# Moving work between the stages of an attention, experts and dense kernel: second routing, first dense tile, early flag, new step order

## The chip, the cores and the metric

The kernel runs on one core of one Trainium2 chip. The metric is the device time of one execution in microseconds (us), the median of several runs. A profile, taken by the hardware profiler in one execution, shows every instruction of five engines: TensorE (PE; its weight loads are PEld), VectorE (DVE), ScalarE (ACT), GpSimd (POOL) and SyncE (SP, which issues most DMAs).

## The reference

Three parts follow each other; 3072 tokens (4 batches of 768) have 384 channels (8 heads of 48).

```
for t in range(S):                       # 1. attention: a complex decaying state per batch and head
    new_re = ar * S_re - ai * S_im       # ar, ai: a_re, a_im scaled to a magnitude of at most 0.999
    new_im = ar * S_im + ai * S_re
    S_re, S_im = new_re + outer(k[t], v[t]), new_im
    y[t] = q[t] @ S_re
logits = x @ w_gate + modality_bias[modality_id]      # 2. experts, one of 8 for each token
e_idx  = argmax(logits); gate_w = softmax(logits)[e_idx]
out[e_idx == e] = gate_w * (relu(x @ w1[e]) @ w2[e])  # 384 -> 1024 -> 384
h = ((x @ w1) * (x @ w2)) @ w3                        # 3. dense, 384 -> 1024 -> 1024
result = h @ w_out                                    # 1024 -> 384
```

The gate and bias weights of part 2 and all four weights of part 3 arrive as 64-bit floats.

## The kernel before

**Stage A, attention.** The sequence is cut into 24 chunks of 128 tokens (4 batches of 6). The decay's magnitudes and angles are prepared for groups of one or two chunks (`f_mag`, L180, and `f_ang`, L240): logarithm, exponential, arctangent and sine on ScalarE, and sums along the sequence as scans on VectorE (L214 for `ar`, L256 for `ai`), with a few products on GpSimd (L218, L261). A chunk itself is a list of 16 named steps, `STEPS`, written by hand: its scores (`sc0`, `sc1`), outputs (`y0`, `y1`) and the writing of its predecessor's rows (`out`, `lg`); for the next chunk the transposes of K and Q in two halves (`kt0`, `kt1`, `qt0`, `qt1`, all in `t_tr`, L320 to L331) and the state (`st1`, `st2`); for the chunk after that the products of q and k with the magnitudes (`mq`, `mk`) and with cosine and sine (`tc`, `ts`, in `t_rot`, L309, which reads the transposes `c` and `s` of L299). The program calls these steps in the list's order; a scheduler may move instructions on PE, DVE and SP within limits. Behind every step a queue of operations with due times is served: the next group's magnitudes and angles, loads, and the **routing** of the first half of the tokens.

**Routing** (`route`, L916) is a generator of 18 pieces. From the logits of 12 chunks it finds each token's expert (L932 to L940), counts tokens with two matmuls (`ct`, `rk`, L945, L946), works out where every token goes (L952 to L990), builds one-hot matrices (`ohB` L994, `ohBx` L997 on ScalarE and L998 on GpSimd, `ohA` L1004) and turns them into lists of row numbers with 12 matmuls (`perm`, L1008). The routing of half 0 is queued in chunk 12 from `R_A` to `R_B`, its names begin with `r0`. That of half 1 (`r1`) runs after the last chunk, in one go:

```
for _ in groups[1][0]:
    pass
g.g2 = g.cp.tile([P, NTILE], F32, name="g2")
setA()
gates(tc, g, g.pa, "", g.g2)
nc.vector.tensor_tensor(g.g2, g.g2, g.g2, ALU.mult)
```

`setA` loads ScalarE's table for exponentials, `gates` (L1017) computes `ex` and the gate factor `g`.

**Stage B, experts.** Each half has two items of 800 rows, each item two subs of 400 rows: 8 subs, the first four for half 0. A sub gathers its rows (`xg`, GpSimd's DMA), transposes them (`xt`, L444), splits them into a high part on ScalarE (`xh`, L445) and a low part on VectorE (`xl`, L446), and then has 8 steps `f`: `h(f)` is 9 matmuls (three terms for each of three slices, L456) with a relu and a split (`hh` L460, `hl` L461), `z(f-2)` 9 more (L474). `zev` takes the sums out, `otr` transposes them (`zo`, L488), copies them (`zr`, L490) and scatters them to a buffer in memory (`zs`, L491, GpSimd's DMA). The next item's weights are split into `wh` and `wl` (L513, L514). Beside that a list `work` of 42 items is popped by progress: 28 of `w34_work` (24 units converted from 64-bit floats, and w3 @ w_out as `w34p`), and 12 units that convert m1 and m2 (`conv_m`, L1206); the conversion is a chain of VectorE instructions (L805 to L818). A step counts as done 48 times (6 steps in each of 8 subs), and the pace is `total * done / (todo * 0.93)` with `todo` 48.

**Stage C, dense** (`c_stage`, L704). Six tiles of 512 tokens: `load` brings four blocks `cz` back from memory, `tr` transposes them (`czt`, L729; `czh` L730, `czl` L731), `ab(f)` computes both products (`ca`, `cb`, L743; `cat` L747, `cab` L749), `o` multiplies with the combined weight (`co`, L764), `ev` scales with the gate and stores.

**End** (`general`, L1327). Two conditions under which the fast path doesn't hold are put into one flag: `okp` (a matmul, a sum over all of `chk`), `fl`, `fi` (L1343), a load of the flag into a register on every engine (L1344), and a branch (L1345).

PSUM has 8 banks of 128 x 2 KB; in stages B and C four of them are the group `ps`, which `xt`, `h`, `zo`, `czt`, `ca` and `cb` share.

Of the kernel before, what the change touches and what calls it, by code (L numbers as in the profile page):

```python
# [55 lines left out]
R_A = 1.2  # L56
# [5 lines left out]
STEPS = ["sc0", "kt0", "mq", "out", "qt0", "sc1", "st1", "mk", "y0", "kt1", "lg", "tc", "y1", "ts", "st2", "qt1"]  # L62
# [519 lines left out]
def attention(tc, g):  # L582
    nc = tc.nc
    g.pa = g.left.enter_context(tc.tile_pool(name="pa", bufs=1, reuse_waits="tile"))
    g.bact = g.right.enter_context(tc.tile_pool(name="bact", bufs=1, side="right", reuse_waits="tile"))
# [66 lines left out]
    start, rest = b_stage(tc, g, groups, work)  # L652
# [51 lines left out]
def c_stage(tc, g):  # L704
    nc = tc.nc
    V, A, TE = nc.vector, nc.scalar, nc.tensor
    ps, pc = g.Cs, g.Cact
# [4 lines left out]
    def load(s):  # L712
        for t in range(CT // P):
            n = s * (CT // P) + t
            b = n // (GB * NCH)
            x = ps.tile([P, DM], F32, tag="zr", bufs=4, name=f"cz{n}")
            d = nc.sync.dma_start(out=x, in_=g.zsv[NRC * b][n * P:(n + 1) * P, :])
            for r in range(1, NRC):
                for q in g.scat[b][r]:
                    tc.add_manual_dep(d.ins, q.name, mybir.DependencyInfo(mybir.DependencyClass.Sync, mybir.DependencyReason.DATA), reason="rows scattered")  # L720
            zt[s, t] = x

    def tr(s):
        hi = ps.tile([P, NTH, CT], R, tag="zh", bufs=2, name=f"czh{s}")
        lo = ps.tile([P, NTH, CT], R, tag="zl", bufs=2, name=f"czl{s}")
# [8 lines left out]
    def ab(s, f):  # L734
# [45 lines left out]
    for s in range(ns):  # L780
        for f in range(1, NF):
            ab(s, f)
            o(s, f - 1)
            if f == 4 and s + 1 < ns:
                tr(s + 1)
                if s + 2 < ns:
                    load(s + 2)
        if s + 1 < ns:
            ab(s + 1, 0)
        o(s, NF - 1)  # L790
        ev(s)
# [124 lines left out]
def route(tc, g, pool, b0, b1, fx, cap, rows, nit, kc, nk_, idx, eid, nt, lidx=None):  # L916
# [81 lines left out]
    nc.gpsimd.tensor_tensor(Bx[:, :, 1, :], Bc, cst[:, C_TB + b0 * NCH:C_TB + b1 * NCH].unsqueeze(2).to_broadcast(shB), ALU.mult)  # L998
# [327 lines left out]
def general(tc, g):  # L1326
# [17 lines left out]
    anyf = nc.values_load(fi[0:1, 2:3], min_val=0, max_val=1)  # L1344
    with tc.If(anyf > 0):  # L1345
# [43 lines left out]
def build(ctx, tc, g):  # L1389
# [7 lines left out]
    with tc.tile_pool(name="Cw", bufs=1, reuse_waits="tile") as Cw:  # L1397
# [20 lines left out]
        g.right.close()  # L1418
        with tc.tile_pool(name="Cs", bufs=1, reuse_waits="tile") as Cs, tc.tile_pool(name="Cact", bufs=1, side="right", reuse_waits="tile") as Cact:
            g.Cs, g.Cact = Cs, Cact  # L1420
            c_stage(tc, g)
# [47 lines left out]
```

## Time and profile before

| | us |
|---|---|
| median of 3 runs | 936.71 (935.76 to 937.67) |
| the profiled execution | 936.86 |
| its span, first to last instruction | 935.0 |
| start-up, before the first chunk | about 0 to 37 |
| stage A with its 24 chunks | about 37 to 333.4 |
| between A and B | 333.4 to 343.8 |
| stage B | 343.8 to 609.3 |
| between B and C | 609.3 to 616.3 |
| stage C | 616.3 to 924.8 |
| end | 924.8 to 935.0 |

The bounds of the stages are those of PE's work: the last `lq` of a chunk, the first `h`, the last `z`, the first `ca`, the last `co`. A view of stretches gives for each the busy time of every engine and the TensorE clock that was granted, 1.00 being 2.4 GHz and 0.50 the lower level, 1.2 GHz. A time in brackets behind an instruction is how long its engine stood idle before it, and what ended that.

### The profile page before, as it was taken

To read this page: it belongs to the slowest core of one execution; us is meant where nothing else is said; L and a number is where in the kernel's file an instruction comes from. 1 tells how busy PE (TensorE), PEld (TensorE's weight loads), DVE (VectorE), ACT (ScalarE), POOL (GpSimd) and SP (SyncE) were. 2 spreads that over 40 slices of the span, in tenths; PEclk is the share of its full clock that TensorE was granted. 3 is DMA by queue.
4 is the path that set the end of the run, shared out by engine and by line. 5 is a ranking of instruction groups with operands and counts; after the bars stand their busy time and mean duration, and the time that the engine had idled before them with its cause. 6 is when DMAs were issued, how large, how long until landed. Compare 5 with 4: busy or idle time off the path is not lost.

```text
span 935.0 us, 14100 instructions
## 1 busy us (share of the span) xinstructions
PE 836.4 (89%) x5469; PEld 760.5 (81%) x5469; DVE 540.6 (58%) x953; ACT 420.6 (45%) x722; POOL 165.7 (18%) x136
## 2 busy tenths in 40 slices
PE   0559889887988969999999999989999999999995
PEld 0548778766777859899999999978888888888884
DVE  2658987889887669877782898223232232222222
ACT  4758888887786423432442443122222122222211
POOL 2213233233234221233231211110000000000000
PEclk9969999988889979999999999999999999999998
DMA  6513443434343334563451354111000010100001
GB/s 159 137 30 105 126 111 100 111 98 140 107 125 95 99 120 144 176 194 117 138 162 33 119 161 120 34 58 34 34 6 28 35 34 35 34 34 1 34 0 39
DMA packets 77951, 81.02 MB, mean 87 GB/s; under 512 B 25704, under 2 KB 70232, under 8 KB 77876
## 3 DMA queue, kind: packets, MB, share of 16 engines
q1 hardware_dynamic: 72324, 70.13, 25.7%
q0 software_dynamic: 5120, 9.70, 3.7%
q8 instruction: 45, 0.74, 0.3%
q14 instruction: 30, 0.25, 0.1%
q10 hardware_dynamic: 432, 0.20, 0.1%
HBM read 65.75 MB, written 14.44 MB: 86 GB/s over the span
## 4 chain that ended last, share of the span: by engine, by line
PE 60%; issue 13%; DVE 10%; POOL 5%; ACT 5%; DMA 2%; POOLq 0%; DVEq 0%; ACTq 0%; SPq 0%
PE ca L743 11%; PE co L764 11%; PE cb L743 11%; PE h L456 6%; PE z L474 6%; PE w34p L868 4%; DVE ar L214 2%; PE sc L364 2%; DVE ai L256 2%; POOL xg L434 1%; POOL zs L491 1%; PE tpk L326 1%; PE sp L340 1%; PE yT L381 1%; POOL ai L261 1%
## 5 line engine op out<-in xcount | busy, mean ns | idle before, releaser
L749 DVE TENSOR_TENSOR cab<-cb,cat 128x512 f32<-128x512 f32 x48 | 33.2, 692 | 182.1 <-PE cb L743 182.1
L747 ACT ACTIVATE cat<-ca 128x512 f32<-128x512 f32 x48 | 28.7, 598 | 123.0 <-PE ca L743 123.0
L752 ACT ACTIVATE cabh<-cab 128x512 fp32r<-128x512 f32 x48 | 30.3, 631 | 94.5 <-DVE cab L749 94.5
L456 PE MATMUL h<-xh,wh 128*128 128x400 f32 x192 | 68.5, 357 | 1.4 <-DVE xl L446 1.2
L456 PE MATMUL h<-xh,wl 128*128 128x400 f32 x192 | 66.8, 348 | 0.0
L456 PE MATMUL h<-xl,wh 128*128 128x400 f32 x192 | 66.8, 348 | 0.0
L474 PE MATMUL z<-hh,wh 128*128 128x400 f32 x192 | 66.8, 348 | 0.0
L474 PE MATMUL z<-hh,wl 128*128 128x400 f32 x192 | 66.5, 346 | 0.0
L474 PE MATMUL z<-hl,wh 128*128 128x400 f32 x192 | 66.1, 344 | 0.0
L460 ACT ACTIVATE hh<-h 128x400 fp32r<-128x400 f32 x64 | 32.2, 503 | 74.4 <-PE h L456 73.2
L764 PE MATMUL co<-w34h,cabl 128*128 128x384 f32 x192 | 65.1, 339 | 0.0
L764 PE MATMUL co<-w34h,cabh 128*128 128x384 f32 x192 | 65.0, 339 | 0.0
L764 PE MATMUL co<-w34l,cabh 128*128 128x384 f32 x192 | 65.0, 339 | 0.0
L491 POOL DMA_INDIRECT zs<-zr,idx x32 | 35.1, 1098 | 161.9 <-ACT zr L490 102.6
L364 PE MATMUL sc<-tq,tk 96*128 96x128 f32 x384 | 58.5, 302 | 0.2 <-ACT tq L331 0.2
L743 PE MATMUL ca<-czh,m1h 128*128 128x512 f32 x144 | 57.3, 398 | 0.4 <-ACT czh L730 0.4
L743 PE MATMUL ca<-czl,m1h 128*128 128x512 f32 x144 | 57.4, 399 | 0.0
L743 PE MATMUL ca<-czh,m1l 128*128 128x512 f32 x144 | 57.3, 398 | 0.0
L743 PE MATMUL cb<-czl,m2h 128*128 128x512 f32 x144 | 56.4, 392 | 0.0
L743 PE MATMUL cb<-czh,m2h 128*128 128x512 f32 x144 | 56.0, 389 | 0.0
L743 PE MATMUL cb<-czh,m2l 128*128 128x512 f32 x144 | 56.0, 389 | 0.0
L364 PEld LDWEIGHTS sc<-tq,tk 96*128 96x128 f32 x384 | 54.1, 218 | 0.9 <-ACT tq L331 0.8
(247 smaller groups left out, 2157.8 us busy)
## 6 DMA issues: line engine op xcount, KB each, us to landing
ws<-in_w SPq DMA_DIRECT2D x32, 384.0 KB, 4.6
w<-in_m3t SPq DMA_DIRECT2D x16, 512.0 KB, 4.1
v<-in_v SPq DMA_DIRECT2D x24, 256.0 KB, 3.1
m<-in_m SPq DMA_DIRECT2D x12, 512.0 KB, 4.1
q<-in_q SPq DMA_DIRECT2D x24, 192.0 KB, 2.6
k<-in_k SPq DMA_DIRECT2D x24, 192.0 KB, 2.6
xb<-xr SPq DMA_DIRECT2D x24, 192.0 KB, 2.2
cz<-zs SPq DMA_DIRECT2D x24, 192.0 KB, 3.5
```

The source lines that it names most:

```text
L214: V.tensor_tensor_scan(t["ar"], g.rst[:, :NTH * GROUPS[n][2] * P], t["s2"], 0.0, ALU.mult, ALU.add)
L364: nc.tensor.matmul(sc[:, j * P:(j + 1) * P], kt[:, j * P:(j + 1) * P], qt[:, j * P:(j + 1) * P], start=True, stop=True)
L456: TE.matmul(p[:, :SUB], lt[:, sl], rt[:, i, :], start=(n == 0), stop=(n == 3 * NTH - 1))
L460: A.activation(hh, p[:, :SUB], AF.Relu)
L474: TE.matmul(acc[j][:, :SUB], lt[:, sl], rt, start=(f == 0 and k == 0), stop=(f == NF - 1 and k == 2))
L491: d = G.indirect_dma_start(out=g.zsv[r_ * NRC + r], out_offset=bass.IndirectOffsetOnAxis(ap=idx[:, c0 + r:c0 + r + 1], axis=0), in_=u, in_ ...
L743: TE.matmul(p, lt[:, i, sl], rt[:, i, :], start=(n == 0), stop=(n == 3 * NTH - 1))
L747: A.activation(at, pr[0], AF.Copy)
L749: V.tensor_tensor(t, pr[1], at, ALU.mult)
L752: A.activation(hi, t, AF.Copy)
L764: TE.matmul(acc[s][t][:, :DM], lt[:, sl], rt, start=(f == 0 and k == 0), stop=(f == NF - 1 and k == 2))
L868: nc.tensor.matmul(ps[:, :DM], a[:, k * P:(k + 1) * P], b_[:, hf * K2 + k, :], start=(hf == 0 and k == 0 and j == 0), stop=(hf == 1 and k ...
```

## The change

Six edits are made together.

1. `STEPS` has another order, and `R_A`, the first due time of half 0's routing, goes from 1.2 to 0.9 of a chunk.
2. Half 1's routing, the table load, the gates and the square go into a list `side` of 20 entries, of which two are popped after each of the first ten steps of stage B. Its small tiles get a pool `rp` of their own. `work` starts only when `side` is empty, and its pace is changed: with `todo` 38 and a divisor of 31.3 steps.
3. In the last sub of stage B the load of the first dense tile is issued at f = 4, and its transposes before the last `z`. `zh` and `zl` come alternately from two pools with one buffer each.
4. `flags`, cut from `general`, runs before the dense tiles.
5. `open_c` closes the pool of the conversions during the last sub.
6. The product at L998 goes from GpSimd to VectorE.

```diff
-R_A = 1.2
+SIDE = 2
+R_A = 0.9
-STEPS = ["sc0", "kt0", "mq", "out", "qt0", "sc1", "st1", "mk", "y0", "kt1", "lg", "tc", "y1", "ts", "st2", "qt1"]
+STEPS = ["sc0", "kt0", "mq", "out", "sc1", "qt0", "mk", "st1", "kt1", "y0", "lg", "tc", "qt1", "y1", "ts", "st2"]
...
-        todo = n * (NF - 2)
+        todo = n * (NF - 2) - R_N // SIDE - 1
...
+                if not nx and f == 4:
+                    assert not work
+                    g.open_c()
+                    g.C[0](0)
...
-                while work and total - len(work) < total * done / (todo * 0.93):
+                for _ in range(SIDE):
+                    if side:
+                        side.pop(0)()
+                while work and not side and total - len(work) < total * (done - R_N // SIDE - 1) / (todo * 0.93 - 4):
                     work.pop(0)()
             x["z"](NF - 2)
             if nx:
                 nx["h"](0)
+            else:
+                g.C[1](0)
             x["z"](NF - 1)
...
-    for _ in groups[1][0]:
-        pass
+    def late():
+        setA()
+        gates(tc, g, g.rp, "", g.g2)
+        nc.vector.tensor_tensor(g.g2, g.g2, g.g2, ALU.mult)
+        rx.close()
...
+    def early():
+        g.rp = rx.enter_context(tc.tile_pool(name="rp", bufs=1, reuse_waits="tile"))
+
+    side.extend([early] + [lambda: next(groups[1][0], None)] * R_N + [late])
...
-    load(0)
-    tr(0)
-    load(1)
-    ab(0, 0)
+    def run():
+        load(1)
+        ab(0, 0)
...
-    nc.gpsimd.tensor_tensor(Bx[:, :, 1, :], Bc, cst[...], ALU.mult)
+    V.tensor_tensor(Bx[:, :, 1, :], Bc, cst[...], ALU.mult)
...
         rest()
+        g.right.close()
+        flags(tc, g)
+        with tc.tile_pool(name="Cact", bufs=1, side="right", reuse_waits="tile") as Cact:
+            g.Cact = Cact
+            g.C[2]()
```

**How the order moves: a chunk of stage A.** This is PE in a chunk in the middle of stage A (chunk 12). `tpq` and `tpk` are transposes of Q and K, `yT` is `y1`, `c` and `pq` are transposes of `t_tok`, `sc` the next chunk's scores. Before:

```order
L420 MATMUL lq_2282<-cst,lts_2182 128x128
L299 MATMUL s_2287<-cst,ai_1396 128x128 x3
L381 MATMUL yT_2257<-pt_2223,v_1658 64x128 x2
L386 MATMUL yT_2257<-tq_2151,S_2015 48x128 x2
L381 MATMUL yT_2257<-pt_2223,v_1658 64x128 x2
L386 MATMUL yT_2257<-tq_2151,S_2015 48x128 x2
L299 MATMUL c_2321<-cst,sn_1704 128x128 x3
L326 MATMUL tpq_2335<-cst,Q_2120 96x128 x4
L364 MATMUL sc_2347<-tq_2205,tk_2169 128x128 x4
```

With the change:

```order
L421 MATMUL lq_2299<-cst,lts_2196 128x128
L300 MATMUL s_2304<-cst,ai_1392 128x128 x3
L327 MATMUL tpq_2315<-cst,Q_2120 96x128 x4
L382 MATMUL yT_2282<-pt_2217,v_1658 64x128 x2
L387 MATMUL yT_2282<-tq_2134,S_2022 48x128 x2
L382 MATMUL yT_2282<-pt_2217,v_1658 64x128 x2
L387 MATMUL yT_2282<-tq_2134,S_2022 48x128 x2
L300 MATMUL c_2336<-cst,sn_1702 128x128 x3
L365 MATMUL sc_2352<-tq_2232,tk_2180 128x128 x4
```

The second half's `tpq` has moved from behind `c` to ahead of `yT`, so `c` stands four transposes later and `sc` where it stood. On VectorE the first routing's cast `r0ohb`, which PE's `ct` needs, moves in the same chunk against the scan of the angles. Before:

```order
L936 SCALAR_TENSOR_TENSOR r0ew<-dl,cst 128x96
L367 TENSOR_TENSOR pt_2223<-sc_2218,cst 128x512
L256 SCALAR_TENSOR_TENSOR ai_1681<-ai_1681,carry_1903 128x256 x3
L938 TENSOR_REDUCE r0m_2195<-r0ew 128x12
L258 TENSOR_SCALAR sn_1975<-ai_1681 128x768
L939 TENSOR_TENSOR r0oh<-r0ew,r0m_2195 128x12x8
L196 SCALAR_TENSOR_TENSOR s_10_2241<-s_10_2242,ar_1951 128x768
L940 CAST r0ohb<-r0oh 128x96
```

With the change:

```order
L958 SCALAR_TENSOR_TENSOR r0ew<-dl,cst 128x96
L960 TENSOR_REDUCE r0m_2153<-r0ew 128x12
L961 TENSOR_TENSOR r0oh<-r0ew,r0m_2153 128x12x8
L962 CAST r0ohb<-r0oh 128x96
L257 SCALAR_TENSOR_TENSOR ai_1677<-ai_1677,carry_1903 128x256 x3
L368 TENSOR_TENSOR pt_2217<-sc_2212,cst 128x512
```

The cast now stands ahead of the scan and of `pt`, `sn` and `s`.

**From A to B.** This is VectorE at the end of stage A (`LG` is the last chunk's logits). Before:

```order
L421 TENSOR_REDUCE LG_94<-lq_3625 128x8
L932 TENSOR_TENSOR r1lgb<-LG_94,bias 128x48
L940 CAST r1ohb<-r1oh 128x96
L1027 RECIPROCAL g_3711<-g_3711 128x24
L698 TENSOR_TENSOR g_3711<-g_3711 128x24
L952 TENSOR_REDUCE r1ne<-r1cts 128x8
L968 SCALAR_TENSOR_TENSOR r1cs__3665<-r1cts 128x96
```

With the change:

```order
L422 TENSOR_REDUCE LG_94<-lq_3625 128x8
L954 TENSOR_TENSOR r1lgb<-LG_94,bias 128x48
L962 CAST r1ohb<-r1oh 128x96
L1049 RECIPROCAL g_3632<-g_3632 128x24
L712 TENSOR_TENSOR g_3632<-g_3632 128x24
L447 TENSOR_TENSOR xl_3645<-xt_3646,xh_3644 128x400
L447 TENSOR_TENSOR xl_3645<-xt_3653,xh_3644 128x400
L447 TENSOR_TENSOR xl_3645<-xt_3660,xh_3644 128x400
L462 SCALAR_TENSOR_TENSOR hl_3686<-h_3675,hh_3685 128x400
```

The three `xl` follow the gate factor `g` directly; the routing's pieces from `ne` on stand behind the first `hl`. The scheduler has left the pieces up to `ohb` and the gates where they were.

**From B to C.** This is PE from the last `z` to the first `ca`. Before:

```order
L474 MATMUL z_6352<-hl_6521,wh_5996 128x400
L488 MATMUL zo_6555<-cst,zt_6551 100x128
...
L488 MATMUL zo_6582<-cst,zt_6551 100x128 x3
L729 MATMUL czt_6611<-cst,cz_6601 128x128
...
L729 MATMUL czt_6625<-cst,cz_6607 128x128
L743 MATMUL ca_6640<-czh_6609,m1h 128x512
```

With the change:

```order
L475 MATMUL z_6376<-hl_6505,wh_6010 128x400
L750 MATMUL czt_6560<-cst,cz_6445 128x128
...
L750 MATMUL czt_6574<-cst,cz_6451 128x128
L475 MATMUL z_6374<-hh_6536,wh_6010 128x400
...
L475 MATMUL z_6376<-hl_6537,wh_6010 128x400
L489 MATMUL zo_6594<-cst,zt_6590 100x128
...
L489 MATMUL zo_6621<-cst,zt_6590 100x128 x2
L1356 LDWEIGHTS tri
L1356 MATMUL okp<-okf,tri 128x48
L764 MATMUL ca_6671<-czh_6558,m1h 128x512
```

The 12 `czt` stand ahead of the last nine `z`, and behind the 12 `zo` only the flag's matmul is left before `ca`.

## Rows read from the trace of the kernel before

**Rows 1.** Stretches: from:to, length; busy PE, PEld, DVE, ACT, POOL; clock; DMA share; GB/s.

```profile
44.00:332.20 288.20, 244.77 (x2344) 211.49 (x2344) 232.82 (x393) 214.29 (x345) 84.58 (x52) 0.90 0.37 103
333.40:343.80 10.40, 3.16 (x26) 3.17 (x27) 8.69 (x42) 2.14 (x6) 0.77 (x1) 0.64 0.34 114
343.80:410.00 66.20, 64.46 (x355) 63.31 (x354) 58.37 (x117) 26.53 (x52) 21.12 (x18) 0.95 0.60 183
410.00:520.00 110.00, 110.00 (x644) 109.23 (x643) 69.77 (x121) 40.00 (x74) 25.98 (x23) 1.00 0.36 109
```

**Rows 2.** PE from A to B: start, us, instruction, [idle before, releaser].

```profile
340.90 0.45 PE L1008 MATMUL r1perm<-r1ohBx,r1ohA 128*100 128x32 bf16 x4 [4.84 <-POOL r1ohBx L998]
...
344.67 0.54 PE L456 MATMUL h<-xl,wh 128*128 128x400 f32 x1
```

**Rows 3.** VectorE and ScalarE from A to B, in order of time.

```profile
334.46 0.36 ACT L151 ACTIVATE ex<-dl 128x192 f32<-128x192 f32 x1 [0.76 <-DVE dl L935]
...
335.53 0.21 DVE L940 CAST r1ohb<-r1oh 128x96 bf16<-128x96 f32 x1
...
335.99 0.18 DVE L698 TENSOR_TENSOR g<-g 128x24 f32<-128x24 f32 x1
```

**Rows 4.** PE and ScalarE from B to C.

```profile
609.26 1.73 PE L488 MATMUL zo<-cst,zt 128*100 128x128 f32 x12
...
614.80 1.09 PE L729 MATMUL czt<-cst,cz 128*128 128x128 f32 x8 [3.16 <-ACT zr L490]
...
619.95 0.40 PE L743 MATMUL cb<-czh,m2h 128*128 128x512 f32 x1
...
622.02 0.39 PE L743 MATMUL ca<-czh,m1h 128*128 128x512 f32 x1
```

**Rows 5.** ScalarE's `zr` from B to C.

```profile
614.25 0.49 ACT L490 ACTIVATE zr<-zo 100x384 f32<-100x384 f32 x1 [3.39 <-DMA zs<-zr,idx]
```

**Rows 6.** VectorE at the end.

```profile
925.42 0.17 DVE L1343 CAST fi<-fl 128x4 int32<-128x4 f32 x1
```

**Rows 7.** Branches and semaphores at the end: engine queue, name, min/mean/max ns, first to last start.

```profile
L1345 PEldq COMPARE_BRANCH  x1: 4422/4422/4422, 926.4 to 926.4; - x1
L1345 DVEq EVENT_SEMAPHORE  x2: 21/21/21, 930.1 to 930.2; - x2
L1345 PEldq EVENT_SEMAPHORE  x2: 51/51/51, 930.9 to 931.1; - x2
```

**Rows 8.** The first routing in stage A, VectorE and GpSimd, and an undisturbed scan.

```profile
218.38 1.80 DVE L940 CAST r0ohb<-r0oh 128x96 bf16<-128x96 f32 x1
...
231.61 0.35 DVE L994 TENSOR_TENSOR r0ohB<-r0col,cst 128x192 bf16<-128x192 f32 x1
231.88 3.38 DVE L214 TENSOR_TENSOR_SCAN ar<-rst,s 128x768 f32<-128x768 f32 x1
233.60 1.96 POOL L998 TENSOR_TENSOR r0ohBx<-r0ohB,cst 128x192 bf16<-128x192 bf16 x1
...
258.14 1.75 DVE L214 TENSOR_TENSOR_SCAN ar<-rst,s 128x768 f32<-128x768 f32 x1
```

**Rows 9.** Waits, stage A, PE: sum, count, longest.

```profile
PE r0ct L945 <- DVE r0ohb L940: 4.9, 1, 4.9
```

**Rows 10.** PE and VectorE in a chunk of stage A.

```profile
250.71 0.60 PE L326 MATMUL tpq<-cst,Q 128*96 128x128 f32 x4
250.91 0.56 DVE L317 TENSOR_TENSOR K<-k,c 128x384 f32<-128x384 f32 x1 [0.49 <-PE c L299]
251.14 1.06 PE L364 MATMUL sc<-tq,tk 96*128 96x128 f32 x8
```

**Rows 11.** VectorE's groups in stage B: xcount, busy, mean ns, idle before and releaser.

```profile
L461 DVE SCALAR_TENSOR_TENSOR hl<-h,hh 128x400 fp32r<-128x400 f32 x64 | 36.5, 570 | 27.1 <-ACT hh L460 26.7
L514 DVE TENSOR_TENSOR wl<-ws,wh 128x768 fp32r<-128x768 f32 x24 | 22.6, 952 | 1.4 <-ACT wh L513 1.4
```

**Rows 12.** PE's stall early in stage B.

```profile
396.48 0.45 PE L456 MATMUL h<-xh,wh 128*128 128x400 f32 x1 [1.23 <-DVE xl L446]
```

More of the change, by code (lines that the diff above doesn't have):

```diff
@@ L523, in b_group, with rt, b_stage @@
     eid = g.cp.tile([P, NIT], I32, name=f"eid{r}")
-    rt = route(tc, g, g.pa, r * GB, (r + 1) * GB, f"r{r}", T, ROWS, NIT, C_KT, 4, idx, eid, g.nts[:, r:r + 1], lidx)
-    return rt, idx, lidx, eid
-def b_stage(tc, g, groups, work):
+    def rt():
+        yield from route(tc, g, g.rp, r * GB, (r + 1) * GB, f"r{r}", T, ROWS, NIT, C_KT, 4, idx, eid, g.nts[:, r:r + 1], lidx)
+    return rt(), idx, lidx, eid
+def b_stage(tc, g, groups, work, side):
     ws = [(r, it, b_weights(tc, g, r, it, groups[r][3])) for r in range(NGR) for it in range(NIT)]
@@ L584, in attention @@
     g.pa = g.left.enter_context(tc.tile_pool(name="pa", bufs=1, reuse_waits="tile"))
+    g.rp = g.pa
     g.bact = g.right.enter_context(tc.tile_pool(name="bact", bufs=1, side="right", reuse_waits="tile"))
@@ L651, in attention @@
     work = []
-    start, rest = b_stage(tc, g, groups, work)
+    side = []
+    start, rest = b_stage(tc, g, groups, work, side)
     put([lambda: next(groups[0][0], None)] * R_N, GB * NCH + R_A, GB * NCH + R_B)
@@ L715, in load @@
             b = n // (GB * NCH)
-            x = ps.tile([P, DM], F32, tag="zr", bufs=4, name=f"cz{n}")
+            x = g.Cs.tile([P, DM], F32, tag="zr", bufs=4, name=f"cz{n}")
             d = nc.sync.dma_start(out=x, in_=g.zsv[NRC * b][n * P:(n + 1) * P, :])
@@ L723, in tr @@
     def tr(s):
-        hi = ps.tile([P, NTH, CT], R, tag="zh", bufs=2, name=f"czh{s}")
-        lo = ps.tile([P, NTH, CT], R, tag="zl", bufs=2, name=f"czl{s}")
+        hi = (g.Cact if s % 2 else g.Cs).tile([P, NTH, CT], R, tag="zh", bufs=1, name=f"czh{s}")
+        lo = (g.Cact if s % 2 else g.Cs).tile([P, NTH, CT], R, tag="zl", bufs=1, name=f"czl{s}")
         for i in range(NTH):
@@ L768, in ev @@
             n = s * (CT // P) + t
-            u = pc.tile([P, DM], F32, tag="ob", bufs=3, name=f"cob{n}")
+            u = g.Cact.tile([P, DM], F32, tag="ob", bufs=3, name=f"cob{n}")
             if t % 2 == 0:
@@ L774, in ev @@
             nc.sync.dma_start(out=g.out[n * P:(n + 1) * P, :], in_=u)
-    load(0)
-    tr(0)
-    load(1)
-    ab(0, 0)
[L780 to L791, printed above, removed]
+    def run():
+        load(1)
+        ab(0, 0)
+        for s in range(ns):
+            for f in range(1, NF):
+                ab(s, f)
+                o(s, f - 1)
+                if f == 4 and s + 1 < ns:
+                    tr(s + 1)
+                    if s + 2 < ns:
+                        load(s + 2)
+            if s + 1 < ns:
+                ab(s + 1, 0)
+            o(s, NF - 1)
+            ev(s)
+    return load, tr, run
 def f64_to_f32(tc, pool, src, n, key, tag, bufs=1, gpool=None):
@@ L1323, in tile, with flags @@
         return ptile(self.g, name, dict(wk="ps", acc="bz")[tag])
-def general(tc, g):
+def flags(tc, g):
     nc = tc.nc
@@ L1343, in general @@
     V.tensor_copy(fi, fl)
-    anyf = nc.values_load(fi[0:1, 2:3], min_val=0, max_val=1)
-    with tc.If(anyf > 0):
+    g.fi = fi
+    g.anyf = nc.values_load(fi[0:1, 2:3], min_val=0, max_val=1)
+def general(tc, g):
+    nc = tc.nc
+    V = nc.vector
+    fi = g.fi
+    with tc.If(g.anyf > 0):
         g.psb = Banks(g)
@@ L1415, in build, with open_c @@
         work += [open_w] + w34_work(tc, g) + [open_m] + [lambda i=i: g.mu[i]() for i in range(4 * NTH)]
-        rest()
+        def open_c():
+            g.cvx.close()
+            g.Cs = g.cvx.enter_context(tc.tile_pool(name="Cs", bufs=1, reuse_waits="tile"))
+            g.C = c_stage(tc, g)
+        g.open_c = open_c
+        rest()
+        g.right.close()
[3 more added lines that the diff above has]
+            g.C[2]()
         g.cvx.close()
[L1418 to L1421, printed above, removed]
         general(tc, g)
```

15 lines of the change are left out of this document (6 added, 9 removed).

## The prediction

> **What bounds the kernel now.** I read the stretches first: they tell in which stage PE has work. In stage A it is busy 244.8 of 288.2 us, VectorE 232.8 and ScalarE 214.3, at a granted clock of 0.90: no engine alone is the bound, and a chunk is as long as the waits between three engines make it. Between A and B PE works 3.16 of 10.40 us. In stage B it is busy nearly throughout (64.5 of 66.2 us, then 110.0 of 110.0) [rows 1]. So time can be had where PE stands still: in A, at the two joins and at the end. Then I read the instructions in order of time at these places, with the waits in brackets. At the first join PE waits 4.84 us for GpSimd's `r1ohBx` before the routing's last matmuls, and the first `h` that needs `xl` begins only at 344.67 [rows 2]. At the second it waits 3.16 us before the last eight `czt` [rows 4], and the `zr` that it waits for stood 3.39 us behind a scatter [rows 5].
>
> **The sum** is made against the profiled execution, 936.86 us; the median of the runs, 936.71, is 0.15 below, which changes nothing.
>
> *From A to B: −7.9.* With the routing gone, `xt` can follow the last logits, since its rows were gathered long before. VectorE still has the head of the routing and the gates ahead of `xl`: their last, `g`, ends at 335.99 + 0.18 = 336.17 [rows 3]. ScalarE has only `ex` ahead of `xh`, which ends at 334.82 [rows 3]. A subtraction of `xl`'s shape takes 0.57 (that of `hl` [rows 11]), so the first `xl` ends at 336.74, and the third `h` matmul starts there instead of at 344.67 [rows 2]: 7.9 us. Bounds: VectorE's 336.17 could hide less if the `xt` come late; half the gain is then left (−4). The other end is −9, since PE's standstill there leaves the first `h` at the lower clock, which a shorter one may not. I take −7.9, which follows from the rows.
>
> *The routing's matmuls in B: +0.9.* They now lie on a busy PE. Four `perm` took 0.45 [rows 2], twelve 1.35; `ct` and `rk`, three times as wide, I take at twice a `perm` each. That is 1.8 us at the clock of this join, 0.64 on average and mostly its lower level [rows 1], and half of it at 2.4 GHz. VectorE could add a wait for `ohb` to it, or PE could hide it in a wait that it has anyway: bounds 0 and +1.8. VectorE's pieces, the table load and the gates lie beside PE's work, as long as VectorE keeps ahead: in the first steps of B, `work` is now empty, so it has room.
>
> *The pace of the conversions: 0.* 42 items are spread over 31.3 steps instead of 44.6 (48 × 0.93), 1.34 in a step for 0.94. Does VectorE keep up? In 343.8 to 410 lie 12 steps of 5.5 us and 11.3 items. VectorE worked 58.4 us, of which 12 `hl` (6.8), 6 `xl` (3.4) and 8 `wl` (7.6) [rows 11] are the stage's own 1.5 a step; 40.5 us are left, 3.6 an item. In 410 to 520 lie 20 steps and 18.8 items: 69.8 less 30 leaves 40, 2.1 an item [rows 1]. Over both an item costs 2.7; at the new pace 1.34 × 2.7 + 1.5 = 5.1 of a step's 5.5. It fits, with little to spare. What it costs when it doesn't is a rival below.
>
> *From B to C: −3.5.* Before, the last `z` gives way to `zo` at 609.26, and nine `ca` and nine `cb` are through when the next `ca` starts, at 622.02 [rows 4]. Now the 12 `czt` stand ahead of the last `z`: 12 × 1.09/8 = 1.6 us, so that `zo` starts at 610.9. Its `zr` still go through two buffers, so the third comes as late behind `zo` as it did: 614.25 + 0.49 − 609.26 = 5.5 [rows 4, 5], at 616.4, while `ca` runs. `cb` needs the PSUM bank that this `zr` empties, and takes 622.02 − 619.95 = 2.1 [rows 4]: through at 618.5, so 3.5 earlier. What is late next is that bank, no longer `czt`. Bounds: −1.5, if `cb` has to wait for the last of the four scatters, and −5.5, if it takes a bank that is free. The loads of `cz` are hidden behind the sub's last four steps, 20 us.
>
> *The end: −0.8.* The flag `fi` is now ready before stage C, not at 925.6 [rows 6]; PE's branch, which took 4.42 us, let go of PE at 930.9, VectorE's at 930.1 [rows 7]. VectorE's last tile keeps its place, so its branch is the last: 0.8 less. Bounds 0 and −4.4, if the branch itself gets shorter. `okp`, one matmul, and six small VectorE instructions stand at the start of C, where `ca` or the bank covers them.
>
> *Stage A: −2.9.* First, `r0ohBx`. GpSimd's multiply ran beside the scan of `ar`, which took 3.38 instead of 1.75 [rows 8], 1.6 lost on VectorE. It moves to VectorE, where I price it by `r0ohB` of the same shape, 0.35 [rows 8]: −1.3. The Trainium skill, "SBUF — State Buffer", "Who interferes with whom", says that a VectorE instruction with two inputs in SBUF and a GpSimd instruction that reads SBUF block each other as wholes, whichever starts second. The 3.38 agrees. The rule also speaks against the edit, since the moved multiply has two such inputs and may itself be blocked by GpSimd's next product. The rows' own bound for that: the cast below was lengthened by 1.6, which would turn −1.3 into +0.3; I keep −1.3, since the scan's loss is seen and the other is not; by the other the sum would be 1.6 higher, 924.3, within the forecast's own bounds. Second, `r0ct`. PE waited 4.9 us for `r0ohb` [rows 9], which stood behind a scan and three more and took 1.80, where `r1ohb` took 0.21 [rows 3, 8]. Now it stands ahead of the scan. VectorE was busy for most of those 4.9 us, and what it had to do it still has; so I count only the cast's lengthening, 1.6. Bounds 0 and −4.9. Third, the order of the steps: 0 of 22 chunks, with a bound on both sides below.
>
> −7.9 + 0.9 − 3.5 − 0.8 − 2.9 = −14.2: 936.9 − 14.2 = 922.7, and I forecast **923**.
>
> **The rivals.**
>
> *The new order makes each chunk longer.* The second half's `tpq` now stands ahead of `yT`, and `c` follows later by it: 251.14 − 250.71 = 0.43 us. VectorE's `K`, which needs `c`, already waited 0.49 [rows 10], and the next transposes, scores and products hang on it. If nothing takes it up, 22 chunks lose 9.5 us: 932. If the added wait also brings the lower clock, at which the same transposes take twice as long, they lose 19: 942. This ends slower than before from the point where a chunk loses over (14.2 + 1.9) / 22 = 0.73 us. For it speaks that VectorE is the busiest beside PE in A and that `c` is on its path; against it, that `sc` keeps its place, that the scores and the state come earlier by as much, and that VectorE's order hardly changes. 0.07 for a loss of that size (0.06 of it more than 0.2% slower than before), 0.08 for a part of it (927 to 934).
>
> *VectorE becomes the bound in B.* The items are not alike: 3.6 us at the start, 2.1 later. Where the first ones are packed, VectorE needs 1.34 × 3.6 + 1.5 = 6.3 in a step of 5.5. Those 11.3 items take 8.4 steps, so it falls behind by 7 us: 930. If all were of that kind, 31 steps would lose 25 us: 948. A single stall is seen in the trace before, PE 1.23 us for `xl` [rows 12] in the dense stretch, and the clock there is 0.95 on average [rows 1]. Against it: PE's own share of the items (`w34p`) is packed as well and makes the steps longer. 0.10 for 930, 0.02 for 948.
>
> *Stage A packs better than counted.* If all 4.9 us of the `r0ct` wait go and a chunk gains 0.12 us, 3.3 + 2.6 more are gone: 917. For it, PE's idle 43 us in A [rows 1] and a clock of 0.90; against it, that three engines share that time. 0.12.
>
> *The first join gives half.* If `xl` waits for something that the routing hid so far, such as the transposes or ScalarE's `xh`, 4 us are lost: 927. 0.09.
>
> **How the numbers follow.** The forecast, with its own bounds (919 to 926), has 0.52; the rivals have the chances given. A measurement here can tell about 0.2% (1.9 us) from no change. Slower by more than that: 0.06 of the first rival and 0.02 of the second, 0.08; within it 0.04, between the slow parts of both; faster 0.88. The range runs from 916, the better-packed A, to 933, both partly slow cases; beyond it lie 0.08 + 0.04 above and some 0.05 below.
>
> **What would show it.** In the profile after: `h` with `xl` should start about 3.3 us after the last `lq` has ended, VectorE's `r1ne` behind the first `hl`, and no `perm` ahead of `xt`. Stage B should be about 1 us longer, with no PE wait for `xl` or `hl` above 1 us; if VectorE is over 95% busy there and PE waits, the pace is the cause. From the last `z` to the end of the first `cb` it should take some 7.6 us, with a wait for `zr`. The scan beside `r0ohBx` should take 1.75. The chunks of stage A should take as long as before: if the 22 are longer and PE waits more for `K`, the step order is the cause, and the forecast falls by what they sum to. It is wrong also if A is shorter by over 6 us.

## The result, and the profile after

The changed kernel takes 927.45 us (median of 4 runs, 925.46 to 927.90), the kernel before in the same comparison 936.24 (934.46 to 937.67, 4 runs): a ratio of 0.990, 95% interval 0.988 to 0.993. The forecast was 923 in a range of 916 to 933; the sign and the range held, of 14.2 us forecast 8.8 came. The profiled execution after took 927.26 us with a span of 925.4, 9.6 less than the 935.0 before. By the marks between the stages the 9.6 falls apart so:

| stretch, and what ends it | before | after | difference | forecast |
|---|---|---|---|---|
| start and stage A, to the last `lq` | 333.04 | 332.40 | −0.6 | −2.9 |
| A to B, to the first `h` with `xl` | 11.63 | 3.89 | −7.7 | −7.9 |
| stage B, to the last `zo` | 264.6 | 269.7, of it 1.2 `czt` | +3.9 | +0.9 |
| B to C, to the second `ca` | 12.8 | 6.3, and the 1.2 `czt` | −5.3 | −3.5 |
| stage C, to the last `co` | 302.4 | 304.1 | +1.75 | 0 |
| end | 10.6 | 9.0 | −1.6 | −0.8 |

A mark is where the named instruction or group begins. The 0.6 of the first row are two things: the first chunk's logits came 2.0 us earlier, at 74.9 instead of 76.9, by which profiles of one and the same order of steps differ too, and from there to the last logits stage A became 1.3 us longer.

Stretches of the changed kernel first, in the columns of [rows 1]:

```profile
44.00:331.70 287.70, 238.10 (x2339) 207.47 (x2338) 227.27 (x393) 213.88 (x345) 83.85 (x51) 0.92 0.38 103
336.30:402.00 65.70, 65.70 (x388) 65.12 (x389) 42.55 (x100) 24.26 (x46) 15.90 (x14) 1.00 0.44 134
402.00:512.00 110.00, 105.13 (x600) 102.60 (x599) 88.52 (x166) 41.43 (x79) 28.73 (x25) 0.98 0.49 144
```

PE's standstill in B, 1.7 us in the first stretch of the kernel before, has moved into the second and grown to 4.9, where VectorE works 88.5 of 110 us instead of 69.8. PE at the joins (order of time, as [rows 2, 4]):

```profile
332.56 1.20 PE L445 MATMUL xt<-cst,xg 100*128 100x100 f32 x12
334.62 0.45 PE L457 MATMUL h<-xh,wh 128*128 128x400 f32 x1 [0.86 <-ACT xh L446]
...
336.29 0.45 PE L457 MATMUL h<-xl,wh 128*128 128x400 f32 x1 [1.05 <-DVE xl L447]
```

```profile
606.03 1.82 PE L489 MATMUL zo<-cst,zt 128*100 128x128 f32 x12
...
608.07 0.50 PE L764 MATMUL ca<-czh,m1h 128*128 128x512 f32 x1
...
610.25 0.39 PE L764 MATMUL cb<-czh,m2h 128*128 128x512 f32 x1
...
612.29 0.39 PE L764 MATMUL ca<-czh,m1h 128*128 128x512 f32 x1
```

The first `h` comes 2 us after the last `lq`, and `cb` follows `ca` without a wait. Waits of PE in B (as [rows 9]), and of VectorE there for the 64-bit weights of the conversions:

```profile
PE w34p L890 <- DVE w34l L900: 4.8, 2, 2.6
DVE cvw L827 <- DMA w<-in_m3t: 6.9, 4, 2.5
```

Waits of PE in A:

```profile
PE tpk L327 <- ACT ys L390: 13.6, 5, 3.2
PE tpk L327 <- DVE K L318: 11.0, 9, 1.9
```

### The profile page after: what moved, and what is told of

It reads as the page before. It is cut to its first block, busy times and chain, and to the rows that moved or that the text cites. A ratio compares the mean times of both kernels' runs of the same rounds, so it can differ in the third digit from the quotient of the medians.

```text
span 925.4 us, 14094 instructions
## 1 busy us (share of the span) xinstructions
PE 827.8 (89%) x5469; PEld 752.2 (81%) x5469; DVE 532.7 (58%) x955; ACT 420.8 (45%) x722; POOL 165.3 (18%) x134
## 4 chain that ended last, share of the span: by engine, by line
PE 65%; DVE 15%; ACT 5%; DMA 5%; issue 2%; POOL 2%; SPq 0%; POOLq 0%; DVEq 0%; ACTq 0%
PE ca L764 11%; PE co L785 11%; PE cb L764 11%; PE h L457 8%; PE z L475 8%; PE w34p L890 3%; PE sc L365 2%; DVE ar L215 2%; POOL ai L262 2%; DMA w<-in_m3t 1%; DVE ai L257 1%; DMA w<-in_mo 1%; PE xp L408 1%; DVE wl L515 1%; PE tpk L327 1%
## 5 line engine op out<-in xcount | busy, mean ns | idle before, releaser
L327 PE MATMUL tpk<-cst,K 128*96 128x128 f32 x192 | 31.4, 289 | 32.5 <-ACT ys L390 13.6
```

The lines of the kernel that those rows point to most:

```text
L327: nc.tensor.transpose(tp[:96, j * P:(j + 1) * P], src[:, hf * 4 + j].rearrange("p a d -> p (a d)"), g.ident)
```

## The experiments

In A the start differs from profile to profile by up to 3.6 us whatever the kernel (the first `LG` lies between 73.3 and 76.9 us). So I measure A from the first `LG` to the last of 24, in three pieces: to the 12th (no routing yet), to the 16th (the first routing), to the last.

| profile | to the 12th | to the 16th | to the last | sum |
|---|---|---|---|---|
| before | 130.1 | 51.0 | 75.4 | 256.5 |
| changed | 133.1 | 46.5 | 78.3 | 257.8 |
| e1, new order alone | 133.3 | 53.1 | 80.0 | 266.3 |
| e2, changed with old order | 130.2 | 46.7 | 78.8 | 255.7 |
| e3, multiply alone | 128.8 | 52.1 | 82.6 | 263.6 |
| e5, due time alone | 130.1 | 46.5 | 79.0 | 255.6 |
| e8, changed, B to end mended | 133.4 | 45.4 | 75.0 | 253.8 |
| e9, e8 with old order | 128.5 | 48.5 | 81.0 | 258.1 |
| e10, product behind scan | 125.8 | 47.0 | 74.7 | 247.5 |
| e11, product on VectorE | 125.2 | 49.8 | 79.9 | 254.8 |
| e12, e10 with old order | 122.1 | 48.3 | 75.6 | 246.0 |

**e1: the new order alone.**

```diff
-STEPS = [..., "out", "qt0", "sc1", "st1", "mk", "y0", "kt1", "lg", "tc", "y1", "ts", "st2", "qt1"]
+STEPS = [..., "out", "sc1", "qt0", "mk", "st1", "kt1", "y0", "lg", "tc", "qt1", "y1", "ts", "st2"]
```

> The kernel before with the new STEPS alone; routing's due time and the GpSimd multiply stay. Theory: the new order itself makes stage A longer, and the changed kernel hid that behind what the first routing gave back. The last lq, at 333.04 in the kernel before, should come 1 to 4 us later (334 to 337), and the time should be 937 to 940. Rival: the order is worth nothing or helps, and the first routing gave less than I counted: last lq at 331 to 333.5, time 935 to 937.

The last `lq` came 6.5 us later than before, more than the theory's 4. The four runs of this kernel lay at 929.8 and at 944.2 to 945.4, so no ratio was formed: the shortest is below both expectations, the others above both, and the whole time decides nothing. I use the first piece of the profile, which is of the run of 944.15: 133.3 us to the 12th `LG`, where the old order takes 128.5 to 130.2 and the new one 133.1 to 133.4 in every profile with the product of L218 and the scan left as they were. That is 0.3 us a chunk. For this piece the rival falls.

**e2: the changed kernel with the old order.**

```diff
-STEPS = [..., "out", "sc1", "qt0", "mk", "st1", "kt1", "y0", "lg", "tc", "qt1", "y1", "ts", "st2"]
+STEPS = [..., "out", "qt0", "sc1", "st1", "mk", "y0", "kt1", "lg", "tc", "y1", "ts", "st2", "qt1"]
```

> The changed kernel with the old STEPS, all else as changed. Theory (the order costs): the first routing's 3 us stay and the order's loss goes, the last lq comes at 328 to 331 instead of 332.40, and the time falls from 927.4 to 924 to 926. Rival (the first routing gains only because the new order puts its cast ahead of the scan): the last lq stays at 332 to 334, time 927 to 929, and PE waits again 4 to 5 us for r0ohb.

924.89 us (923.65 to 929.30), ratio 0.990 (0.986 to 0.994): the last `lq` at 329.9, PE's wait for `r0ohb` 1.2 us. The theory holds for the first routing, whose gain doesn't need the order. The ratio is that of the changed kernel, so the order's loss isn't seen in the whole time, and of the theory only the stage's part is shown.

**e3: the multiply alone.**

```diff
-    nc.gpsimd.tensor_tensor(Bx[:, :, 1, :], ...
+    V.tensor_tensor(Bx[:, :, 1, :], ...
```

> The kernel before with the multiply of r0ohBx and r1ohBx on VectorE alone. Theory: the scan of ar beside the first one takes 1.75 us instead of 3.38, the multiply itself about 0.35, and the last lq comes about 1.3 us earlier, at 331.7; between A and B the wait for r1ohBx (4.84 us) falls by about 0.8, to 4. In all 2 us faster. Rival (VectorE's multiply waits for GpSimd's products instead): the multiply takes over 1.5 us and the last lq stays within 0.5 us of 333.04.

One run, 942.67 us: the last `lq` came at 338.9, 5.9 us later than before, and between A and B it took 11.6 us as before, with a wait of 4.7 for `r1ohBx`. VectorE and GpSimd at the place of [rows 8]:

```profile
230.43 3.38 DVE L214 TENSOR_TENSOR_SCAN ar<-rst,s 128x768 f32<-128x768 f32 x1
233.73 0.33 DVE L998 TENSOR_TENSOR r0ohBx<-r0ohB,cst 128x192 bf16<-128x192 bf16 x1
...
230.32 1.86 POOL L218 TENSOR_TENSOR ai<-ai,s 128x768 f32<-128x768 f32 x1 [7.31 <-ACT s L151]
```

Both are wrong. The multiply takes 0.33 us, as I priced it, but the scan still takes 3.38. What lengthens it isn't `r0ohBx`: it is the product at L218, which began 0.11 us ahead of it. The scan runs on for its own 1.75 us from about the product's end, 232.18. In the kernel before it stood the same: product at 231.77 for 1.86, scan at 231.88. Why this one run lost 7 us in A isn't shown.

**e4: the second routing in 5 steps, the conversions over 36.**

```diff
-SIDE = 2
+SIDE = 4
```

> The changed kernel with SIDE = 4: the second routing takes 5 steps instead of 10, and the conversions get 36 steps instead of 31.3. Theory: the two waits of PE for w34l (4.8 us together, with the lower clock behind them) come from VectorE's packed conversions; at 1.17 items a step instead of 1.34 they are gone or below 1 us in all, stage B gets 4 to 5 us shorter, time 922 to 924. Rival (they come from where the units stand beside the weights of the next item, or from the DMA that VectorE waited for, not from the pace): a wait of 2 us or more for w34l or w3h stays, time 926 to 928.

924.57 us (919.01 to 925.94), ratio 0.986 (0.982 to 0.991). One wait for `w34l` of 3.8 us stayed, and B took 270.8 instead of 269.7: the rival. The mean pace isn't what stops PE. The wait now lay one sub earlier, at 419.8 to 423.7, where no weights are split, but behind a sub that splits some: VectorE was still busy in 15.2 of the 16 us up to there.

**e5: the due time alone.**

```diff
-R_A = 1.2
+R_A = 0.9
```

> The kernel before with R_A = 0.9 alone. From the 12th to the 16th of the logits' LG (the chunks with the first routing) the kernel before took 51.0 us, the changed one 46.5, the new order alone 53.1, the multiply alone 52.1. Theory: the earlier due time alone brings the gain, since it sets the cast r0ohb ahead of the scan: 46 to 48 us, PE's wait for r0ohb below 1.5 us. Rival: only the due time together with the multiply brings it; then 49 to 52 us, and the scan beside r0ohBx still takes over 3 us. Whole time 930 to 935 or 935 to 937.

The pieces say theory: 46.5 us for 51.0, with GpSimd's multiply in place and a wait for `r0ohb` of 1.2. The multiply and the scan lay side by side, and the scan took 1.75:

```profile
225.14 3.25 POOL L998 TENSOR_TENSOR r0ohBx<-r0ohB,cst 128x192 bf16<-128x192 bf16 x1 [4.42 <-DVE r0ohB L994]
...
226.33 1.75 DVE L214 TENSOR_TENSOR_SCAN ar<-rst,s 128x768 f32<-128x768 f32 x1
```

Here the multiply is the one that was held, 3.25 us where `r1ohBx` of the same shape takes 0.77, although by its record it began first; another VectorE instruction (`s`, from 224.98) was running when it did. The whole time is the rival's: 936.31 us in 10 runs for 935.67 in 13, ratio 1.001 (0.999 to 1.003). The last piece took 79.0 instead of 75.4. So 4.5 us were gained at the routing, and in the profile 3.6 were lost behind it.

**e6: the odd tiles elsewhere, a fourth output buffer.**

```diff
-        hi = (g.Cact if s % 2 else g.Cs).tile(..., tag="zh", ...
+        hi = (g.Cs2 if s % 2 else g.Cs).tile(..., tag="zh", ...
...
-            u = g.Cact.tile([P, DM], F32, tag="ob", bufs=3, name=f"cob{n}")
+            u = g.Cact.tile([P, DM], F32, tag="ob", bufs=4, name=f"cob{n}")
```

> The changed kernel with the transposed tiles of odd number in a pool beside that of the even ones instead of among stage C's working tiles, and with four output buffers instead of three. Theory for stage C: where the odd tiles lie makes PE's ca and cb 3% slower there (6.32 us a step instead of 6.25); stage C from the second ca to the last co takes 302.4 as in the kernel before, instead of 304.1. Rival: it is the change of pool between tiles or the tiles themselves; 304.1 stays. Theory for the end: the last output block waited 2.76 us for a store to free a buffer; with a fourth the wait is gone, and from the last co to the end it takes 6.2 to 7 us instead of 9.0. Rival: the stores' queue or the branch sets the end, 8.5 to 9. Whole time 923 to 924 under both theories.

Stage C took 302.3 us, as the theory says. The end took 7.5: the wait is gone, but the theory's 6.2 to 7 isn't reached. The chain of work in an odd tile of the changed kernel, and in that tile of e6 (start, length, what):

```profile
870.29 2.12 PE ca L764 x9
872.41 2.10 PE cb L764 x9
```

```profile
868.95 2.08 PE ca L764 x9
871.03 2.05 PE cb L764 x9
```

VectorE's last output block in the changed kernel, and in e6:

```profile
919.10 0.62 DVE L794 TENSOR_SCALAR cob<-co,g 128x384 f32<-128x384 f32 x1 [2.76 <-DMA out<-cob]
```

```profile
914.91 0.62 DVE L794 TENSOR_SCALAR cob<-co,g 128x384 f32<-128x384 f32 x1 [0.44 <-PE co L785]
```

The whole time, 919.59 (907.5 to 923.8), lies below the 923 to 924 named for it and spreads more than these 3 us, which the stages show alone. Two edits were made together here; the pool is read from the matmuls, the buffer from VectorE's wait.

**e7: the sums taken out one item earlier.**

```diff
-    stages = (w34_d, w34_c, w34_b, w34_a, w34_l)
+    stages = (w34_c, w34_d, w34_b, w34_a, w34_l)
+    ago = (3, 3, 2, 1, 0)
```

> The changed kernel in which the sums of w3 @ w_out are taken out in the item that ends their matmuls, one item earlier than now. Theory: PE waits for w34l (4.8 us in two waits) because VectorE takes the sum behind the next items' conversions; taken earlier, the waits fall below 1 us in all, and stage B (third h to the last zo, 269.7) gets 4 to 7 us shorter, the lower clock behind the waits included. Rival: VectorE is behind as a whole in those steps; the wait moves to another reader (hl, xl, w3l) and stage B gains under 2 us.

926.52 us (920.8 to 929.2), ratio 0.988 (0.982 to 0.993). The rival: 5.0 us of waits for `w34l` stayed, B took 271.4. VectorE is behind as a whole there.

**e8: conversions by the load of the step.** From e6:

```diff
-SIDE = 2
+SIDE = 4
+W_LO, W_HI = 0.8, 1.4
...
+                if not side:
+                    acc += W_LO if s % 2 and nx and s + 2 < n else W_HI
...
-                while work and not side and total - len(work) < total * (done - R_N // SIDE - 1) / (todo * 0.93 - 4):
+                while work and total - len(work) < acc:
```

> The kernel of e6 (odd tiles beside the even ones, four output buffers) with SIDE = 4 and the conversions popped by weight: 0.8 items a step in the subs 1, 3 and 5, in which VectorE also splits the next item's weights, 1.4 in the others. Theory: PE's waits for w34l (3.8 to 5.0 us in the runs with an even pace, whatever the pace and wherever the sum is taken out) come from a step in which conversions and weight splits meet on VectorE; with the load evened no wait above 1 us stays, and stage B (third h to the last zo, 269.7 to 271.5 in the runs so far) takes 262 to 266. Rival: PE waits for w34l because its one PSUM bank and the order of the units force it; then 3 us or more of such waits stay, 268 to 272. Whole time 913 to 919 under the theory, 919 to 924 under the rival.

917.78 us (907.95 to 922.86), ratio 0.978 (0.974 to 0.982). PE's waits in B:

```profile
PE h L458 <- DVE xl L448: 0.7, 1, 0.7
PE w34p L894 <- DVE w3l L844: 0.6, 1, 0.6
```

B took 265.7. The theory's numbers came: not the mean pace stopped PE, but how the conversions lie over the subs. That it is their meeting with the splits of the next item's weights on VectorE isn't shown alone: VectorE also waited for the conversions' 64-bit weights, 8.7 us in the changed kernel's stage B, 3.9 in e4, 4.6 here and 1.3 before, and 4.5 of the 8.7 lie in the 33 us up to the end of the second stall. e8 changes both; e4, which waited as little and still stalled, speaks for the meeting.

**e9: e8 with the old order** (the edit of e2).

> The kernel of e8 with the old STEPS. Theory: the old order takes 130.1 us from the first LG to the twelfth where the new one takes 133.1 to 133.4, and the first LG comes about 1 us later (73.7 to 76.9 for 73.3 to 74.9); from the first LG to the last 255.5 to 256 instead of 257 to 258; the whole time 1 to 3 us below e8. Rival: the later chunks give it back, as they gave back the earlier due time of the first routing (e5), and the two times agree within 1 us.

920.31 us (918.0 to 924.5), ratio 0.984 (0.981 to 0.987). To the 12th `LG` 128.5, to the last 81.0: the rival, and more than given back.

**What the later chunks give back** is seen at one place in the profile of the changed kernel, around the last scan of `ar` (VectorE, ScalarE, PE):

```profile
278.08 3.25 DVE L215 TENSOR_TENSOR_SCAN ar<-rst,s 128x768 f32<-128x768 f32 x1
281.26 0.52 DVE L318 TENSOR_TENSOR K<-k,s 128x384 f32<-128x384 f32 x1
...
282.17 0.54 DVE L318 TENSOR_TENSOR K<-k,c 128x384 f32<-128x384 f32 x1
...
281.37 0.21 ACT L152 ACTIVATE ec<-ar 128x6 f32<-128x6 f32 x1 [2.25 <-DVE ar L215]
281.49 0.83 ACT L152 ACTIVATE ep<-ar 128x768 f32<-128x768 f32 x1
282.22 0.58 ACT L390 ACTIVATE ys<-yT 128x512 f32<-128x512 f32 x1
...
282.86 0.61 PE L327 MATMUL tpk<-cst,K 128*96 128x128 f32 x4 [3.15 <-ACT ys L390]
```

The scan is lengthened by 1.5 us. ScalarE waits for it at `ec`, and behind `ec` on the same engine stands `ys`, for which PE's next `tpk` waits by the profile. But `tpk` transposes `K`, and `K` stands behind the same scan on VectorE: it ended at 282.71, `ys` at 282.80. So an earlier `ys` would bring 0.1 us here, and the same holds at the other four waits for `ys`. The kernel before had this scan at 284.24 with 1.75 us, behind its product, and its `tpk` waited 0.20. In all 84 pairs of 128x768 that overlap in stage A, in the eleven profiles from the kernel before to e9, the one that begins behind the other's start is the longer: products of up to 3.6 us, scans of 2.5 to 3.4. Which of them it is changes with any shift.

**e10: the product behind the scan.** From e8:

```diff
-        V.tensor_tensor_scan(t["ar"], g.rst...
+        t["scan"] = V.tensor_tensor_scan(t["ar"], g.rst...
...
-        G.tensor_tensor(t["ai"], t["ai"], t["s1"], ALU.mult)
+        x = G.tensor_tensor(t["ai"], t["ai"], t["s1"], ALU.mult)
+        tc.add_manual_dep(x.ins, t["scan"].ins.name, ...)
```

> The kernel of e8 in which GpSimd's product of ai with s (L219 of the changed kernel) waits for VectorE's scan of ar in the same group. In the runs so far a scan takes 1.75 us when it starts first, and then the product takes 3.0 to 3.6 instead of 1.82; when the product starts first, the scan takes 2.5 to 3.4. Theory: with the product always behind, all scans take 1.75, the lengthened ones (3.0 us in all in e8, 4.5 in the changed kernel, 6.1 in the kernel before) are gone, the wait of PE for tpk on ScalarE's ys or tq (1.6 in e8, 3.2 in the changed kernel) falls below 1 us, and from the first LG to the last it takes 250 to 253 us instead of 253.8 (257.8 in the changed kernel). Whole time 911 to 916. Rival: the angles come later by the wait and take back what the scans gain: 254 to 258 us from LG to LG, whole time 917 to 922.

908.36 us (905.58 to 909.44), ratio 0.971 (0.969 to 0.974): the fastest kernel, and faster than both given. VectorE and GpSimd:

```profile
222.65 1.75 DVE L216 TENSOR_TENSOR_SCAN ar<-rst,s 128x768 f32<-128x768 f32 x1
...
224.63 1.92 POOL L220 TENSOR_TENSOR ai<-ai,s 128x768 f32<-128x768 f32 x1 [11.53 <-DVE ar L216]
```

In stage A all eleven scans take 1.75, the products 1.8 to 1.9, and A is 247.5 us from `LG` to `LG`, 6 less than in e8 and below the theory's own range. PE's waits for `ys`:

```profile
PE tpk L329 <- ACT ys L392: 7.4, 5, 1.7
```

They fall from 12.2 us in e8 (13.6 in the changed kernel), not below 1: what I had taken for the whole wait was only the last of five.

**e11: the product on VectorE.** From e8:

```diff
-        G.tensor_tensor(t["ai"], t["ai"], t["s1"], ALU.mult)
+        V.tensor_tensor(t["ai"], t["ai"], t["s1"], ALU.mult)
```

> The kernel of e8 with that product on VectorE instead of GpSimd. Theory (the two engines block each other; VectorE is the busiest beside PE): all scans take 1.75 us, but VectorE gets ten products of about 0.95 us, more than the 3 to 6 us of lengthened scans it loses: 254 to 260 us from the first LG to the last, whole time 917 to 924. Rival (what costs is only that VectorE is held at the wrong moment, and it has room): 250 to 253 us, whole time below 916.

914.90 us (910.13 to 918.69), ratio 0.979 (0.976 to 0.982). The scans take 1.75 here too, and from `LG` to `LG` it takes 254.8, the theory's range; the whole time lies in the rival's and can't be told from e8's. To the 12th `LG` it gains as much as e10, 125.2 us for 125.8, and behind it the gain is lost. So over the stage VectorE pays with the products what it saves at the scans, and of the two remedies only the order of the two brings the whole gain.

**e12: e10 with the old order** (the edit of e2).

> The kernel of e10 (no lengthened scans) with the old STEPS. From the first LG to the twelfth the new order took 133.1 to 133.4 us with lengthened scans and 125.8 without, the old one 128.5 to 130.2 with them. Theory: what the new order lost there came from scan and product meeting differently, not from c standing behind tpq; without the meetings the old order takes as long as the new, 125 to 127, and the whole time is within 3 us of e10's 908.4. Rival: the new order itself costs 0.3 us a chunk, by c behind tpq; then the old order takes 121 to 123.5 us there and the whole time is 904 to 906.

To the 12th `LG` 122.1 us, the rival's range; the whole time, 909.51 (906.89 to 914.10), ratio 0.974 (0.971 to 0.976), the theory's. Without any lengthened scan the new order still costs 3.7 us over eleven chunks, and the later ones return 2.2 of it. Between e10 and e12 the whole time shows no difference.

**Where the new order loses** the traces show, though no run was made for it. In the program of the new order VectorE has the scan of `ar` directly ahead of `K` in seven of eleven groups, in that of the old order in three; the four others lie between 108 and 182 us, in the first piece (in e11 the product stands between the two). One of them in the kernel before, and in the changed one (VectorE, PE):

```profile
136.99 0.54 DVE L317 TENSOR_TENSOR K<-k,c 128x384 f32<-128x384 f32 x1
139.85 2.92 DVE L214 TENSOR_TENSOR_SCAN ar<-rst,s 128x768 f32<-128x768 f32 x1
...
137.58 0.64 PE L326 MATMUL tpk<-cst,K 128*96 128x128 f32 x4 [0.32 <-DVE K L317]
```

```profile
136.58 1.76 DVE L215 TENSOR_TENSOR_SCAN ar<-rst,s 128x768 f32<-128x768 f32 x1
...
139.16 0.55 DVE L318 TENSOR_TENSOR K<-k,c 128x384 f32<-128x384 f32 x1
...
139.85 0.61 PE L327 MATMUL tpk<-cst,K 128*96 128x128 f32 x4 [3.25 <-ACT ys L390]
```

`K` ended at 139.71, `ys` at 139.79. PE's waits before `tpk`, nearly all ended within 0.15 us of the end of `K`, sum to 17.3 us in the first piece of the changed kernel and 11.2 in the kernel before, 13.4 in e10 and 7.3 in e12: 6 us more with the new order both times.

## Why the prediction was right or wrong

**A to B: right.** −7.7 for −7.9, by the path named: VectorE's head of the routing, the gates, then `xl`. Every profile with this edit has 3.9 us in this stretch, every one without it 11.6 to 11.7. The doubt about the clock went the good way: it reads 1.00 in the 66 us behind the join, 0.95 before [rows 1], and what that is worth lies in stage B.

**B to C: the move of `czt` right, the next wait wrong.** I let `cb` wait for the bank behind the third `zr`. That `zr` ended at 611.6, 5.6 us behind the first `zo`, as reckoned with 5.5, but `cb` had begun at 610.25. So the bound "if it takes a bank that is free", −5.5, was the case: −5.3 with the `czt`, for −3.5. The `czt` themselves took 1.2 us (603.08 to 604.31) for 1.6.

**The end: right in sign, by another path.** I took PE's branch for what came last in the kernel before. Behind it came GpSimd's DRAIN, which took 5.29 us in both kernels (min/median/max ns, first to last start):

```profile
L1464 POOLq DRAIN  x3: 40/107/5294, 928.9 to 934.7; - x3
L1501 POOLq DRAIN  x3: 40/107/5294, 617.7 to 925.1; - x3
```

Before, it began behind GpSimd's own branch at 928.9 and ended at 934.2, while PE's semaphores were through at 931.1; with the early flag it lies beside stage C. So the 0.8 that I read from the two branches isn't what was gained. Now VectorE and SyncE come last, VectorE's last block having waited 2.76 us for an output buffer; e6 takes that away and gains another 1.5 us. Forecast −0.8, measured −1.6.

**Stage B: the step that failed is "It fits, with little to spare".** In the mean it fitted with room: 88.5 us of VectorE's work in 110, 4.4 a step where I had 5.1. But the sum averaged over steps that aren't alike: in the subs 1, 3 and 5 the splits of the weights meet the conversions, the weights to convert come late, and VectorE was behind and held `w34l` back, for PE 2.2 and 2.6 us. Around and behind the second wait the clock shows 0.92 (450 to 456 us) and 0.80 (456 to 462). That is my second rival's mechanism at under half of its 7 us, though not its reason: e4 with a slower pace stalls as well, e8 with an evened one doesn't. The routing's matmuls were sized about right: the twelve `perm` took 0.69 us, `ct` and `rk` 0.2 each, overlapping.

**Stage C: not in the forecast.** +1.75 us since odd tiles' transposed inputs moved to the pool of the working tiles: in the three odd tiles nine `cb` take 2.10 us and nine `ca` mostly 2.10, in the even ones 2.05 and 2.08, and in e6, with a pool of their own, 2.05 and 2.08 in all six. What in that pool slows them isn't shown.

**Stage A: three terms, and none came as named.** From the first logits to the last the stage became 1.3 us longer instead of 2.9 shorter; the −0.6 in the table comes from the start. The multiply (−1.3) was priced right and gave nothing: the step that failed is "GpSimd's multiply ran beside the scan of `ar`". The rows showed two GpSimd instructions beside that scan, and I took the one that the change moved; the product had begun first. The Trainium skill, "SBUF — State Buffer", "Who interferes with whom", says that a VectorE instruction with two inputs in SBUF and a GpSimd instruction that reads SBUF block each other, and that the order in which they start decides who is held. The trace agrees with both halves: 3.38 us for the scan that started second, 2.85 for the product that did, 1.75 and 1.82 alone. I had quoted the rule and not asked which of the two had started first. That the scan beside the moved multiply took 1.75 in the changed kernel, as I had named for a sign, was luck: there it began at 229.98, ahead of its product at 230.49. The early cast (−1.6) was undersized at its place: the first routing gave 4.5 us (e5), where PE's wait fell from 4.9 to 1.2, and e5 shows it to be the due time's doing. Over the whole stage 0.9 of it was left in e5's profile, and in the whole time nothing. The order (0) costs 0.3 us a chunk, 3 to 4 us over the first eleven, near the 0.43 of my first rival; e12 shows that it is the order itself. The step that failed is "VectorE's order hardly changes": the scan of `ar` moved ahead of `K` in four more groups, and PE's waits before `tpk` grew from 16.6 to 30.9 us over the stage, the sign that I had named. That `c` comes later, the rival's reason, isn't it: VectorE waited for `c` before `K` 1.5 us in all before and 0.7 after.

That the range held is in part luck: of 14.2 us only the 7.9 of the first join came by the path and in the size named, 2.0 of the profile's 9.6 come from the start, and the surplus at the second join and the end stood against the losses in B and C.

What the terms leave open is why gains in A don't add up. e5's 4.5 us and the order's loss both shrink in the later chunks; the scans that lengthen with any shift are one reason, which e10 removes. Why the first piece gains 7.5 us there and the other two lose 1.3, and why e1's runs differ by 15 us, wasn't tried.

## What to carry to other kernels

Where two engines hold each other up, look at who started first before blaming a partner (and, as in e5, at what else was running), and look at the same pair in every place where it meets; here one instruction ordered behind another brought 6 us in stage A. A wait is put down to what ended last: look at what else the instruction reads, and when that was ready. A budget for background work belongs to each step, with what else that step does on the same engine, not to the mean. A gain in a stage without a single bound counts only once the end of that stage has moved in several runs.

## What the runs showed of the hardware that was not expected

The same matmuls of 512 columns ran 1 to 2% slower for two tiles of one shape at the same granted clock, 1.00: nine `ca` mostly took 2.10 us instead of 2.08, nine `cb` 2.10 instead of 2.05, when the moving tile lay in the other pool.

GpSimd's DRAIN at the end of the program took 5.29 us whether it began at 928.9, where the end waited for it, or at 617.7.

Behind the branch past `general` (L1374 of the changed kernel, L1345 of the one before) PE's record is 3.5 to 4.4 us long, those of the other engines 0.05 to 0.07. That doesn't make the others quick: VectorE, ScalarE and SyncE began their next instruction 2.5 to 3.6 us behind the branch (VectorE's branch is at 919.8, its next instruction at 923.1), GpSimd 0.4 us. What fills that time isn't shown.

The start, up to the first chunk's logits, varies by some 3 us between profiles of kernels whose code up to there is alike.
